# Seven joined block products for the last tokens of two batch pairs

## The chip, the cores and the metric

The kernel runs on one core of a Trainium2 chip. The metric is the device time of one execution in microseconds (us); lower is better. Below, PE is TensorE, DVE is VectorE, ACT is ScalarE, POOL is GpSimd and SP is SyncE.

## What is computed

The inputs are q, k and v of shape (8, 8, 576, 64): batch, heads, tokens, head dimension. A linear attention with a root-mean-square norm feeds a gated linear unit with a causal convolution of five taps:

```python
kv  = einsum('bhsd,bhse->bhde', k, v)
x   = einsum('bhsd,bhde->bhse', q, kv)
x   = x / sqrt(mean(x * x, -1) + 1e-6) * g_norm      # then heads side by side: (8, 576, 512)
gate = sigmoid(sum over k of conv_w[k] * x shifted by 4 - k tokens)
out  = (gate * (x @ w_val)) @ w_out                  # (8, 576, 512)
```

All of it is float32.

## The kernel before

The order of all work is written out by hand: `PLAN` is a list of 1245 steps, `name arguments @ buffers`, and the kernel's last loop calls the function of each step in turn. An engine runs its own instructions in that order; what stands between two engines is a wait for a semaphore. `@ 3 2` picks the numbered buffers of a step's new tiles: eight PSUM banks, and rooms in on-chip memory (`ot` has four, `gate` four, `xs` four, `w64` three, `x` three; `v0`, `v1`, `k0`, `k1` have one each and hold halves of one batch's v and k).

The batches go through these stages, overlapped with one another:

- `kv_product b i` (L478) multiplies k^T v, `kv_copy` takes the result out of PSUM; `load_q` and `turn_q` bring q and transpose it.
- `raw_pair b c` and `raw_tail b` (L553) multiply q by it, in 64x64 tiles, for two chunks of 128 tokens and for the last 64 tokens. `square`, `sums`, `powers` (POOL) and `normalise` (ACT, L638) make x.
- `turn_blocks` and `move_blocks` (L671, DMAs on SP's and POOL's queues) or, for the last 64 tokens, `turn_x` and `keep_x`, put x transposed into `xTs`. `halo` copies the tokens that the convolution reads from before a block.
- `gate_start`, `gate_tap` (L688, one DVE instruction per tap), `gate_end` make the gate of one quarter (128) of the channels.
- `val_fast b mj n` (L749) and `val_keep` make x @ w_val, `gated b jt` (L713) multiplies it by the gate, in place, in `gv`. `gv` holds three batches.
- the second product, w_out, goes by pairs of batches: pair i is batches 2i and 2i + 1. The first 512 tokens of a batch are four chunks of 128. Two chunks and two halves of w_out form two by two blocks, and seven products instead of eight give the result: `fast_product i p n` (L843), n = 0 to 6, p = 0 to 3 (two chunks each, p = 0, 1 of the first batch, 2, 3 of the second). Four of the seven use sums made by `token_sums i h m` (L818), for both p of a batch at once, and sums of weights made once. `fast_keep i p n` copies (n = 0, 1, 2, 6, on ACT, L856, L858, L860, L871) or adds (n = 3, 4, 5, on DVE, L854) what lies in PSUM into two `ot` tiles, and `store` sends these out with four DMAs each (L883).
- the last 64 tokens of the two batches of a pair together are 128 rows, chunk 8: `out_product i 8` (L787) makes them with plain products of 64 columns by 512, `keep_out` (L795) copies, `store i 8` sends.

All four pairs are done so. In PSUM, the b and c results of one (i, p) share a bank, except for (3, 3), the last. `store_last` and `store_part` split the last stores over SP's and ACT's queues.

Of the kernel before, what the change touches and what calls it, by code (L numbers as in the profile page):

```python
# [12 lines left out]
ALU = mybir.AluOpType  # L13
# [18 lines left out]
narrow_weight wval 1 0 @ 0; raw_half 0 1 0 @ 5; square 0 4 @ 0; sums 0 2; narrow_weight wval 0 3;
raw_half 0 1 1; sums 0 4; load_half v 2 1 @ 0; start_warm 2 384 @ 0; narrow_weight wval 1 1;
narrow_weight wval 0 4; powers 0 2; square 0 1 @ 1; narrow_weight wval 1 5 @ 0; narrow_weight wval 1 2;
narrow_weight wval 0 7; stage_weight wout 0 @ 2; turn_q_rows 1 3 @ 7; normalise 0 3 @ 0;
narrow_weight wval 1 3; turn_q_rows 1 2 @ 6; sums 0 1; sort_q 1 3 @ 1; turn_q_rows 1 1 @ 0;
load_half v 2 0 @ 0; narrow_weight wval 2 0 @ 1; turn_x 0 3 @ 1; narrow_weight wval 1 6 @ 1; powers 0 1;
normalise 0 4 @ 1; narrow_weight wval 2 1; turn_q_rows 1 0 @ 7; load_q 2 2; normalise 0 2 @ 2; turn_x 0 4 @ 4;
keep_x 0 3; narrow_weight wval 1 4; turn_x 0 2 @ 3; keep_x 0 4; narrow_weight wval 2 2;
narrow_weight wval 2 5 @ 2; kv_product 1 1 @ 1 4; narrow_weight wval 1 7; keep_x 0 2;  # L40
narrow_weight wval 2 6 @ 3; sort_q 1 1; val_product 0 1 1 @ 3; narrow_weight wval 3 0 @ 0;
narrow_weight wval 3 5 @ 0; halo 0; normalise 0 1 @ 0; narrow_weight wval 3 1; normalise 0 0 @ 1;
narrow_weight wval 2 3; narrow_weight wval 3 6 @ 1; turn_x 0 1 @ 0; narrow_weight wval 3 2; turn_x 0 0 @ 5;
narrow_weight wval 2 4; load_half k 2 1 @ 0; val_product 0 0 1 @ 2; keep_x 0 1; narrow_weight wout 1 5 @ 2;
keep_x 0 0; narrow_weight wval 2 7; narrow_weight wval 3 3; narrow_weight wout 1 0 @ 1;
narrow_weight wout 1 6 @ 0; gate_start 0 0 @ 0; kv_product 1 0; narrow_weight wval 3 4; gate_start 0 3 @ 1;
gate_tap 0 0 3; sort_q 1 2; turn_q_rows 1 4 @ 0; narrow_weight wval 3 7; val_product 0 0 0 @ 5; load_q 2 0;
gate_tap 0 0 2; keep_val 0 0 1; gate_tap 0 3 3; gate_start 0 1 @ 2; sort_q 1 4; val_sums 2;
val_product 0 3 0 @ 6; gate_tap 0 1 3; kv_copy 1 1; kv_copy 1 0; load_q 2 1; sort_q 1 0; gate_tap 0 0 1;
raw_tail 1 @ 0 2; gate_tap 0 3 2; raw_pair 1 3 @ 1 4; square 1 4 @ 2; narrow_weight wout 0 5 @ 3;  # L50
keep_val 0 0 0; gate_tap 0 0 0; val_product 0 2 1 @ 7; gate_start 0 2 @ 3; gate_tap 0 3 1; square 1 3 @ 0;
square 1 2 @ 1; sums 1 4 @ 1 1; gate_tap 0 2 3; narrow_weight wout 1 1; powers 1 4; load_half k 2 0 @ 0;
val_product 0 1 0 @ 5; sums 1 3; keep_val 0 1 1; stage_weight wout 3 @ 0; gate_end 0 0; gate_tap 0 1 2;
powers 1 3; narrow_weight wout 1 2; sums 1 2; narrow_weight wout 1 3; val_product 0 2 0 @ 3; gated 0 0;
keep_val 0 3 0; keep_val 0 2 1; gate_tap 0 2 2; normalise 1 4 @ 2; powers 1 2; narrow_weight wout 1 4;
normalise 1 3 @ 0; raw_pair 1 1 @ 7 6; turn_q 2 0 @ 0; stage_weight wout 2 @ 1; turn_q 2 2; turn_x 1 4 @ 0;
load_q 2 3; val_product 0 3 1 @ 2; gate_tap 0 3 0; keep_x 1 4; normalise 1 2 @ 1; gate_tap 0 2 1;
narrow_weight wout 0 6 @ 2; turn_x 1 3 @ 0; keep_val 0 3 1; gate_tap 0 1 1; load_q 3 1; turn_x 1 2 @ 1;
keep_val 0 1 0; square 1 1 @ 2; kv_product 2 0 @ 4 2; narrow_weight wout 0 0 @ 0; keep_x 1 3;
narrow_weight wout 1 7; keep_x 1 2; sums 1 1; kv_product 2 1; narrow_weight wout 0 1; gate_tap 0 1 0;  # L60
powers 1 1; square 1 0 @ 0; val_product 1 1 1 @ 5; narrow_weight wout 2 0 @ 1; load_half k 3 1 @ 0;
narrow_weight wout 0 2; narrow_weight wout 2 5 @ 1; load_half k 3 0 @ 0; narrow_weight wout 3 5 @ 3;
narrow_weight wout 0 3; sums 1 0; kv_copy 2 0; gate_tap 0 2 0; kv_copy 2 1; narrow_weight wout 2 1;
normalise 1 1 @ 2; powers 1 0; val_product 1 0 1 @ 0; narrow_weight wout 2 6 @ 0; narrow_weight wout 0 4;
turn_q 2 1; val_product 1 3 1 @ 1; halo 1; narrow_weight wout 2 2; narrow_weight wout 0 7; load_q 3 0;
keep_val 0 2 0; turn_q 2 3; keep_val 1 1 1; keep_val 1 0 1; weight_sums 0; normalise 1 0 @ 0; turn_x 1 1 @ 4;
load_q 3 2; narrow_weight wout 3 0 @ 0; raw_pair 2 3 @ 3 2; narrow_weight wout 3 6 @ 1; val_sums 0;
narrow_weight wout 2 3; raw_pair 2 1 @ 5 0; turn_q 3 1 @ 1; square 2 2 @ 1; turn_x 1 0 @ 6; square 2 3 @ 2;
narrow_weight wout 2 4; keep_x 1 1; val_product 1 2 1 @ 7; sums 2 2 @ 0 0; load_half v 3 0 @ 0; keep_x 1 0;
val_sums 1; gate_end 0 3; powers 2 2; load_half v 3 1 @ 0; sums 2 3; keep_val 1 3 1; gate_end 0 1; gated 0 3;  # L70
val_product 1 0 0 @ 4; gate_start 1 0 @ 0; narrow_weight wout 2 7; gate_end 0 2; powers 2 3; gated 0 1;
square 2 0 @ 0; gate_tap 1 0 3; val_product 1 1 0 @ 6; square 2 1 @ 1; turn_q 3 0; normalise 2 2 @ 1;
gated 0 2; load_q 3 3; val_product 1 2 0 @ 1; gate_tap 1 0 2; keep_val 1 2 1; keep_val 1 1 0; sums 2 1;
normalise 2 3 @ 2; load_q 4 0; turn_q 3 2; powers 2 1; val_product 1 3 0 @ 7; sums 2 0;
narrow_weight wout 3 1; token_sums 0 0 0 @ 2; keep_val 1 2 0; narrow_weight wout 3 2; turn_blocks 2 3;
kv_product 3 0 @ 2 6; powers 2 0; gate_tap 1 0 1; narrow_weight wout 3 3; token_sums 0 0 2 @ 1;
keep_val 1 3 0; fast_product 0 0 1 @ 3; normalise 2 1 @ 0; load_half k 4 0 @ 0; narrow_weight wout 3 4;
token_sums 0 0 1; fast_product 0 1 0 @ 1; turn_blocks 2 2; normalise 2 0 @ 2; fast_product 0 0 0 @ 7;
turn_q 3 3; kv_product 3 1; narrow_weight wout 3 7; load_q 4 2; fast_keep 0 0 1 @ 2; keep_val 1 0 0;
token_sums 0 0 3; fast_keep 0 0 0 @ 3; raw_tail 2 @ 0 5; gate_start 1 3 @ 1; turn_blocks 2 1;  # L80
fast_product 0 0 3; square 2 4 @ 2; turn_blocks 2 0; kv_copy 3 1; kv_copy 3 0; gate_start 1 1 @ 2;
fast_product 0 1 1 @ 4; sums 2 4; move_blocks 2 0; weight_sums 1; fast_keep 0 1 0 @ 0; raw_pair 3 1 @ 6 2;
weight_sums 2; powers 2 4; gate_tap 1 1 3; move_blocks 2 2; fast_product 0 0 2; gate_tap 1 0 0;
move_blocks 2 1; fast_product 0 1 2; gate_tap 1 3 3; fast_keep 0 0 2; fast_keep 0 1 1 @ 1; weight_sums 3;
fast_product 0 0 5; move_blocks 2 3; fast_keep 0 1 2; gate_tap 1 1 2; square 3 0 @ 1; fast_product 0 1 4;
# [845 lines left out]
```

## Time and profile before

| | us |
|---|---|
| median of 3 runs | 294.84 (294.74 to 295.19) |
| profiled execution, its own time | 295.31 |
| its span, first to last instruction | 293.5 |
| last instruction of the last k^T v (L478) ends | 190.7 |
| last `gated` ends on VectorE | 274.66 |
| last TensorE record starts | 288.9 |

Granted TensorE clock: 1.000. A float32 matmul of the program shows as two records on TensorE. Records overlap, so the time of a group is read from its start to the start of the next group. Rows of the timeline give start, length and group; rows of groups give the number of instructions, busy time and mean length in ns, and the idle time of the engine ahead of them with what ended it.

### The profile page before, as it was taken

The numbers are of one execution on the slowest core, as the hardware profiler recorded it, in microseconds if no ns is written. First come the engines' busy times: TensorE is split into PE (matmuls) and PEld (weight loads), VectorE is DVE, ScalarE is ACT, GpSimd is POOL, SyncE is SP. The second block draws the span as 40 slices with busy tenths as digits, with TensorE's granted clock in tenths as the row PEclk, the third lists the DMA queues.
The fourth block names the chain that finished last, engine by engine and source line by source line (L and its number), as shares of the span: only waits on it lengthen the run. The fifth ranks groups of instructions, "written<-read, shape, count | busy, mean of one in ns | idle before, by whom it ended". The sixth has DMA issues, their size and how long they took to land.

```text
span 293.5 us, 8687 instructions
## 1 busy us (share of the span) xinstructions
PE 285.4 (97%) x3281; PEld 225.4 (77%) x3281; DVE 268.6 (92%) x484; ACT 198.6 (68%) x621; POOL 122.3 (42%) x131
## 2 busy tenths in 40 slices
PE   6999999999999999999999999999999999999994
PEld 3777778877887868878887767888887588888583
DVE  1699999999999999999999999999998999999812
ACT  2899999999786767876477576658598434723330
POOL 3067064754594378322881748031592072000020
PEclk9999999999999999999999999999999999999999
DMA  7999999968586856947699689624552170221334
GB/s 262 379 388 409 288 252 271 276 223 237 152 223 174 253 129 189 339 129 202 167 252 282 145 233 296 209 61 120 134 129 74 47 170 0 57 54 36 97 102 125
DMA packets 32202, 55.51 MB, mean 189 GB/s; under 512 B 6231, under 2 KB 14679, under 8 KB 32161
## 3 DMA queue, kind: packets, MB, share of 16 engines
q1 hardware_dynamic: 29424, 49.50, 57.7%
q0 software_dynamic: 1760, 3.43, 5.2%
q10 hardware_dynamic: 976, 2.03, 1.9%
q8 instruction: 26, 0.43, 0.6%
q14 instruction: 16, 0.12, 0.1%
HBM read 39.21 MB, written 9.44 MB: 166 GB/s over the span
## 4 chain that ended last, share of the span: by engine, by line
PE 71%; ACT 10%; DVE 9%; DMA 5%; issue 1%; POOL 1%; SPq 1%; ACTq 0%; DVEq 0%
PE bank L843 29%; PE bank L749 28%; PE bank L787 5%; ACT x L638 4%; DMA v<-in_v_dram 4%; PE bank L478 4%; DVE gate L688 4%; PE bank L553 3%; PE bank L565 1%; DMA out_dram<-ot 1%; POOL rt L619 1%; DVE ss L609 1%; SPq L883 1%; DVE ot L424 1%; ACT gv L709 1%
## 5 line engine op out<-in xcount | busy, mean ns | idle before, releaser
L619 POOL TENSOR_TENSOR rt<-ss,mhalf 128x8 f32<-128x8 f32 (+3 forms) x38 | 73.0, 1935 | 78.7 <-DVE ss L609 78.6
L688 DVE SCALAR_TENSOR_TENSOR gate<-xT,cwT,gate 128x576 f32<-128x576 f32 x128 | 100.5, 808 | 0.2
L638 ACT ACTIVATE x<-bank,rt 128x64 f32<-128x64 f32 x252 | 55.8, 366 | 4.0 <-POOL rt L619 3.7
L843 PE MATMUL bank<-wsum,w 128*128 128x256 f32 x192 | 47.6, 381 | 0.1
L671 POOL DMA_DIRECT2D xT<-y x48 | 26.5, 557 | 41.5 <-DVE gv L756 13.5
L843 PEld LDWEIGHTS bank<-wsum,w 128*128 128x128 f32 x192 | 36.0, 190 | 6.4 <-issue 0.8
L749 PE MATMUL bank<-xs,vsum 128*128 128x288 f32 x144 | 37.1, 407 | 0.0
L749 PEld LDWEIGHTS bank<-xs,vsum 128*128 128x128 f32 x144 | 27.3, 190 | 7.3
L700 PE MATMUL bank<-xT,wval 128*128 128x288 f32 x128 | 32.5, 408 | 0.0
L843 PE MATMUL bank<-wout,gv 128*128 128x256 f32 x128 | 32.0, 381 | 0.0
L700 PEld LDWEIGHTS bank<-xT,wval 128*128 128x128 f32 x128 | 23.7, 190 | 6.2 <-ACT xT L657 0.2
L695 ACT ACTIVATE gate<-gate 128x576 f32<-128x576 f32 x32 | 23.0, 725 | 7.9 <-DVE gate L688 7.8
L843 PEld LDWEIGHTS bank<-wout,gv 128*128 128x128 f32 x128 | 24.1, 190 | 3.5
L602 ACT ACTIVATE sq<-bank 128x256 f32<-128x256 f32 (+1 forms) x70 | 21.7, 401 | 6.2 <-PE bank L553 5.8
L682 ACT ACTIVATE gate<-xT,cwT 128x576 f32<-128x576 f32 x32 | 25.2, 803 | 0.9 <-DVE gv L713 0.9
L749 PE MATMUL bank<-xT,wval 128*128 128x288 f32 x96 | 25.7, 406 | 0.0
L713 DVE TENSOR_TENSOR gv<-gv,gate 128x576 f32<-128x576 f32 x32 | 23.5, 747 | 2.0 <-ACT gate L695 1.4
L609 DVE TENSOR_REDUCE ss<-sq 128x8 f32<-128x520 f32 (+1 forms) x40 | 24.8, 625 | 0.3 <-ACT sq L602 0.3
L854 DVE TENSOR_TENSOR ot<-bank,ot 128x256 f32<-128x256 f32 (+1 forms) x33 | 17.4, 535 | 8.0 <-PE bank L843 4.0
L749 PEld LDWEIGHTS bank<-xT,wval 128*128 128x128 f32 x96 | 18.2, 190 | 4.5
L860 ACT COPY ot<-bank 128x256 f32<-128x256 f32 x16 | 6.0, 375 | 22.2 <-PE bank L843 22.2
L678 POOL COPY xT<-xT 128x124 f32<-128x124 f32 x32 | 18.7, 622 | 4.7 <-ACT xT L657 3.5
(91 smaller groups left out, 466.5 us busy)
## 6 DMA issues: line engine op xcount, KB each, us to landing
qs<-in_q_dram SPq DMA_DIRECT2D x96, 140.0 KB, 4.0
out_dram<-ot SPq DMA_DIRECT2D x134, 64.0 KB, 1.7
k<-in_k_dram SPq DMA_DIRECT2D x14, 576.0 KB, 5.1
v<-in_v_dram SPq DMA_DIRECT2D x12, 576.0 KB, 5.3
xT<-y SPq DMA_DIRECT2D x48, 64.0 KB, 2.7
xT<-y POOLq DMA_DIRECT2D x48, 64.0 KB, 2.6
y<-in_moe_w_val_dram SPq DMA_DIRECT2D x4, 512.0 KB, 12.6
w<-in_moe_w_out_dram SPq DMA_DIRECT2D x4, 512.0 KB, 8.1
```

Of the source, the lines that this page charges most:

```text
L602: nc.scalar.activation(out=sq[:, r * n // 2:(r + 1) * n // 2, 0:D], in_=raw.rearrange("p (h e) -> p h e", e=D), func=AF.Square)
L609: nc.vector.reduce_sum(out=st["ss", b][:, FIRST[c]:FIRST[c] + n], in_=st["sq", b, c][:, 0:n], axis=AX.X)
L619: nc.gpsimd.tensor_tensor(out=st["rt", b][:, which], in0=st["ss", b][:, which], in1=mhalf[:, which], op=ALU.pow)
L638: nc.scalar.activation(out=x[:, to * D:(to + 1) * D], in_=raw[:, h * D:(h + 1) * D], func=AF.Copy, scale=root[:, to:to + 1])
L671: (nc.sync if i % 2 else nc.gpsimd).dma_start(out=xTs[b % 2][i * TB:(i + 1) * TB, :, first:first + P], in_=y[a * TB:(a + 1) * TB, i])
L682: nc.scalar.activation(out=gate[:], in_=xTs[b % 2][:, jt, HALO:SX], func=AF.Copy, scale=cwT[:, K - 1, jt:jt + 1])
L688: nc.vector.scalar_tensor_tensor(out=gate[:], in0=xTs[b % 2][:, jt, tap * TB:tap * TB + S], scalar=cwT[:, tap, jt:jt + 1], in1=gate[:], op ...
L695: nc.scalar.activation(out=gate[:], in_=gate[:], func=AF.Sigmoid)
L700: nc.tensor.matmul(val[:], wval[:, kc, jt * P:(jt + 1) * P], xTs[b % 2][:, kc, HALO + n * SV:HALO + (n + 1) * SV], start=(kc == 0), stop=( ...
L713: nc.vector.tensor_tensor(out=both, in0=both, in1=st["gate", b, jt][:], op=ALU.mult)
L749: nc.tensor.matmul(st[bank, "val", b, mj][:], weights_[:, k], tokens()[:, k], start=(n in (0, 1, 3) and k == 0), stop=(k == NK // 2 - 1), ...
L843: nc.tensor.matmul(st[bank, i, p], tokens()[:, k], weights_[:, k], start=((n < 2 or n == 3 and ("bc", i, p) not in st) and k == 0), stop=( ...
```

## The change

Everything up to `kv_product 7 0`, the last k^T v, keeps its order on every engine. Behind it:

- `out_product`, `keep_out` and `store` of chunk 8 are gone for pairs 2 and 3. Instead `keep_tail b` (ACT) copies the last 64 tokens of batches 4 to 7 from `gv` into two tiles of 128 tokens (in `k0` and `k1`), and these two form one more group of two by two blocks, called pair 5, p = 0: four `token_sums`, seven `fast_product`, six `fast_keep` and the stores of two tiles.
- the output sums of (1, 3), (2, 3), (3, 1) and (5, 0) stand in `v0` and `v1` instead of `ot`.
- `move_blocks` is split into a step for POOL's queue and a step for SP's, so that the plan can place them apart.
- all steps behind `kv_product 7 0` have a new order.

```diff
     FAST_OUT = 0
     PAIRED_Q = (0, 1)
+    SPARE = ((1, 3), (2, 3), (3, 1), (5, 0))
+    APART = ((B // 2 - 1, 2 * NV - 1),)
...
-    def move_blocks(b, a):
+    def move_blocks(b, a, e):
...
-        for i in range(HB):
-            (nc.sync if i % 2 else nc.gpsimd).dma_start(
+        for i in range(1 - e, HB, 2):
+            (nc.gpsimd if e else nc.sync).dma_start(
...
+    def keep_tail(b):
+
+        i = b // 2
+        if ("tail", i) not in st:
+            st["tail", i] = new(("wexp", "wexp", "k0", "k1")[i], [P, NK, P], FP32, f"tail{i}")
+        first = b % GVS * S + SF
+        nc.scalar.copy(out=st["tail", i][:, :, b % 2 * T:(b % 2 + 1) * T], in_=gv[:, :, first:first + T])
...
+        if i < B // 2:
+            block = lambda r, k: gv[:, k, begin:begin + SF].rearrange(
+                "p k (m r t) -> p k m r t", m=2, r=2)[:, :, :, r, :]
+            done = lambda m: st["sums", i, h, m // 2][:, m % 2]
+        else:
+            block = lambda r, k: st["tail", 2 * (i - B // 2) + r][:, k]
+            done = lambda m: st["sums", i, h, m // 2][:, m % 2, :, 0]
...
-        chunk = lambda r, k: lambda: gv[:, k, begin + r * P:begin + (r + 1) * P]
+        chunk = lambda r, k: lambda: (
+            gv[:, k, begin + r * P:begin + (r + 1) * P] if i < B // 2 else st["tail", 2 * (i - B // 2) + r][:, k])
...
-        elif bank != "a" and (i, p) == (B // 2 - 1, 2 * NV - 1):
+        elif bank != "a" and (i, p) in APART:
...
-            st["ot", i, 2 * p + row] = new("ot", [P, C], FP32, f"ot{i}_{2 * p + row}")
+            tag = f"v{row}" if (i, p) in SPARE else "ot"
+            st["ot", i, 2 * p + row] = new(tag, [P, C], FP32, f"ot{i}_{2 * p + row}")
...
+            first = 2 * i
+            if i >= B // 2:
+                first, bb, n = 4 * (i - B // 2) + 2 * c, j // 2, NJ * HB + j % 2
```

Pieces of the new order that the prediction speaks of, first around batch 7's raw products and batch 5's gates:

```diff
+fast_product 1 2 3; gate_tap 5 2 1; store 1 5; val_fast 6 1 0 @ 0; val_fast 6 0 1 @ 1; x_sums 6 1 @ 0;
+fast_keep 1 2 5; store 1 4; val_keep 6 1 0; gate_tap 5 2 0; gate_end 5 2; turn_blocks 7 3; turn_blocks 7 2;
+turn_blocks 7 1; move_blocks 7 3 1; move_blocks 7 3 0; gated 5 2; val_fast 6 0 2; gated 5 3; x_sums 6 2 @ 1;
```

and from the last gates to the end (the end before was `... fast_product 3 3 6; fast_keep 3 3 5; store_last 3 6 1; store_last 3 6 0; fast_keep 3 3 6; store_part 3 7 0 1 2 4; store_part 3 7 0 0 0 2`):

```diff
+val_keep 7 1 3; gate_tap 7 2 0; gate_end 7 0; fast_product 3 1 5; fast_product 3 0 3; gated 7 1; gated 7 0; gated 7 3;
+fast_product 3 3 0 @ 0; gate_end 7 2; gated 7 2; keep_tail 7; fast_keep 3 3 0 @ 3; fast_product 3 2 0 @ 5;
+fast_keep 3 2 0 @ 0; token_sums 3 1 0 @ 2; fast_product 3 2 1 @ 4; fast_keep 3 1 5; store 3 2; token_sums 5 0 0 @ 1;
...
+fast_keep 5 0 6; store_last 5 1 1; fast_keep 3 3 6; fast_product 5 0 5; store_last 5 1 0; fast_product 5 0 3;
+fast_keep 5 0 5; store_part 3 7 0 1 2 4; fast_product 3 3 3 @ 7; fast_keep 3 3 3; store_part 3 7 0 0 0 2;
+store_last 5 0 0; store_last 5 0 1; fast_product 3 3 5; fast_keep 3 3 5; store_last 3 6 1; store_last 3 6 0
```

More of the change, by code (lines that the diff above doesn't have):

```diff
@@ L52 @@
[L52 to L60, printed above, removed]
+load_q_rows 0 1; load_q_rows 0 0; load_half v 0 0 @ 0; load_half k 0 0 @ 0; load_half v 0 1 @ 0; load_half k 0 1 @ 0;
@@ L70 @@
[L70 to L74, printed above, removed]
@@ L80 @@
[L80 to L84, printed above, removed]
@@ new lines @@
+token_sums 0 0 1; fast_product 0 1 0 @ 1; turn_blocks 2 2; normalise 2 0 @ 2; fast_product 0 0 0 @ 7; turn_q 3 3;
+kv_product 3 1; narrow_weight wout 3 7; load_q 4 2; fast_keep 0 0 1 @ 2; keep_val 1 0 0; token_sums 0 0 3;
+fast_keep 0 0 0 @ 3; raw_tail 2 @ 0 5; gate_start 1 3 @ 1; turn_blocks 2 1; fast_product 0 0 3; square 2 4 @ 2;
+turn_blocks 2 0; kv_copy 3 1; kv_copy 3 0; gate_start 1 1 @ 2; fast_product 0 1 1 @ 4; sums 2 4; move_blocks 2 0 1;
+move_blocks 2 0 0; weight_sums 1; fast_keep 0 1 0 @ 0; raw_pair 3 1 @ 6 2; weight_sums 2; powers 2 4; gate_tap 1 1 3;
@@ L100 @@
-gated 1 3; turn_blocks 3 1; raw_tail 3 @ 3 4; kv_product 4 0; val_keep 2 1 6; gated 1 2; square 3 4 @ 0;
-turn_blocks 3 2; out_product 0 8 @ 1; sums 3 4; kv_copy 4 1; kv_copy 4 0; turn_blocks 3 3; val_keep 2 0 6;
-powers 3 4; gate_start 2 0 @ 2; token_sums 0 1 0 @ 0; move_blocks 3 2; gate_start 2 2 @ 1; turn_q 4 3;
-normalise 3 4 @ 2; move_blocks 3 1; turn_q 4 1; gate_tap 2 3 3; raw_pair 4 3 @ 2 7; token_sums 0 1 1;
-move_blocks 3 0; gate_tap 2 2 3; raw_pair 4 1 @ 6 5; square 4 3 @ 2; gate_tap 2 2 2; keep_out 0 8 @ 0;
@@ L120 @@
-normalise 4 2 @ 1; val_fast 3 1 4; gate_tap 2 3 0; store 0 7; fast_keep 0 2 5; val_fast 3 0 1 @ 6; turn_q 5 2;
-gate_end 2 3; kv_product 5 1 @ 0 5; x_sums 3 3 @ 3; gate_start 3 0 @ 1; gated 2 3; raw_tail 4 @ 7 2;
-load_half k 6 1 @ 0; kv_product 5 0; gated 2 1; square 4 4 @ 1; store 0 4; val_keep 3 0 1; sums 4 4;
-val_fast 3 0 5; turn_q 5 0; powers 4 4; kv_copy 5 0; fast_keep 0 2 6; gate_start 3 1 @ 0;
-token_sums 1 0 0 @ 1; fast_product 1 1 0 @ 0; turn_blocks 4 2; token_sums 1 0 1; load_q 5 3;
@@ L145 @@
[L145 to L148 removed]
+x_sums 2 0 @ 0; val_fast 2 0 0 @ 0; fast_keep 0 1 5; x_sums 2 1 @ 1; store 0 2; raw_pair 3 3 @ 1 2; val_keep 2 0 0;
@@ new lines @@
+val_fast 2 0 3 @ 3; normalise 3 3 @ 1; val_keep 2 1 4; load_q 4 3; val_keep 2 0 4; val_fast 2 0 5; gate_tap 1 3 1;
+val_keep 2 0 3; val_fast 2 0 6; gate_tap 1 3 0; val_fast 2 1 6; gated 1 1; load_q 5 1; gate_end 1 3; val_keep 2 0 5;
+normalise 3 2 @ 0; kv_product 4 1 @ 6 5; gated 1 3; turn_blocks 3 1; raw_tail 3 @ 3 4; kv_product 4 0; val_keep 2 1 6;
+gated 1 2; square 3 4 @ 0; turn_blocks 3 2; out_product 0 8 @ 1; sums 3 4; kv_copy 4 1; kv_copy 4 0; turn_blocks 3 3;
+val_keep 2 0 6; powers 3 4; gate_start 2 0 @ 2; token_sums 0 1 0 @ 0; move_blocks 3 2 1; move_blocks 3 2 0;
@@ new lines @@
+val_fast 3 1 1 @ 6; sums 4 2; gate_tap 2 1 1; powers 4 2; val_fast 3 0 4; val_keep 3 1 1; turn_blocks 4 3;
+val_keep 3 1 2; val_fast 3 1 5; gate_tap 2 1 0; gated 2 2; fast_product 0 2 5; gate_end 2 1; val_keep 3 1 5;
+fast_keep 0 3 6; normalise 4 2 @ 1; val_fast 3 1 4; gate_tap 2 3 0; store 0 7; fast_keep 0 2 5; val_fast 3 0 1 @ 6;
+turn_q 5 2; gate_end 2 3; kv_product 5 1 @ 0 5; x_sums 3 3 @ 3; gate_start 3 0 @ 1; gated 2 3; raw_tail 4 @ 7 2;
+load_half k 6 1 @ 0; kv_product 5 0; gated 2 1; square 4 4 @ 1; store 0 4; val_keep 3 0 1; sums 4 4; val_fast 3 0 5;
@@ new lines @@
+gated 4 2; square 6 2 @ 1; sums 6 3; turn_q 7 0 @ 1; fast_product 1 3 0 @ 6; load_q 7 2; kv_copy 7 1;
+token_sums 2 0 0 @ 1; fast_product 2 1 0 @ 1; sums 6 2; kv_copy 7 0; token_sums 2 0 1; keep_tail 4 @ 0;
+token_sums 2 0 2 @ 0; turn_blocks 6 0; gate_start 5 3 @ 2; fast_product 2 0 0 @ 5; fast_product 2 0 1 @ 0;
+fast_keep 1 3 0 @ 0; fast_keep 2 1 0 @ 0; gate_start 5 0 @ 3; store 1 8; fast_product 2 1 1 @ 4; fast_keep 2 0 0 @ 1;
+fast_product 2 0 2; fast_product 2 1 2; powers 6 3; token_sums 1 1 1; fast_product 1 3 2; normalise 6 3 @ 2;
@@ new lines @@
+gate_tap 5 0 2; normalise 7 2 @ 0; fast_product 1 3 5; fast_keep 1 3 4; sums 7 3; store 2 3; gate_tap 5 0 1;
+store 2 0; raw_tail 7 @ 2 7; square 7 4 @ 0; gate_tap 5 1 1; store 2 1; fast_product 1 3 6; fast_keep 1 3 6;
+gate_tap 5 0 0; gate_end 5 0; gate_tap 5 1 0; fast_product 1 2 2; fast_keep 1 2 2; halo 6; store 1 7; sums 7 4;
+fast_product 1 2 1 @ 5; gate_end 5 1; fast_keep 1 2 1 @ 2; turn_blocks 7 0; gated 5 0; gate_start 6 3 @ 3; gated 5 1;
+fast_product 1 3 3; fast_keep 1 3 5; powers 7 3; gate_tap 5 3 3; powers 7 4; store 1 6; gate_tap 5 2 3;
```

335 lines of the change are left out of this document (159 added, 176 removed).

## The prediction

> **What bounds the kernel now.** I read the page first (shares of the engines, then the slices), then the busy time by stretches behind the last k^T v, then TensorE's timeline there, the waits, and the end of the chain.
>
> ```profile
> span 293.5 us, 8687 instructions
> PE 285.4 (97%) x3281; PEld 225.4 (77%) x3281; DVE 268.6 (92%) x484; ACT 198.6 (68%) x621; POOL 122.3 (42%) x131
> ...
> PE   6999999999999999999999999999999999999994
> ...
> DVE  1699999999999999999999999999998999999812
> ```
>
> TensorE (PE) and VectorE (DVE) are both near full, and DVE empties only in the last two slices. All steps up to the last k^T v (`kv_product 7 0`) are issued in the same order on every engine after the change, so the first 190.66 us can't differ. The stretches behind it:
>
> ```profile
> core 0: us, PE busy (x) PEld busy (x) DVE busy (x) ACT busy (x) POOL busy (x), PEclk, DMA share, GB/s
> 190.66:200.00 9.34, 9.34 (x50) 8.25 (x44) 9.30 (x18) 6.04 (x20) 3.33 (x2) 1.00 0.33 87
> ...
> 260.00:270.00 10.00, 10.00 (x47) 8.60 (x46) 10.00 (x18) 3.35 (x8) 0.00 (x0) 1.00 0.20 51
> ...
> sum 98.64, PE 98.54 PEld 78.53 DVE 87.68 ACT 50.89 POOL 26.31; mean PE 9.85 PEld 7.85 DVE 8.77 ACT 5.09 POOL 2.63
> ...
> 188.66:274.66 86.00, 85.94 (x649) 70.43 (x640) 83.51 (x139) 49.05 (x144) 24.26 (x31) 1.00 0.33 83
> ```
>
> PE is busy in 98.54 of the 98.64 us from the last k^T v to its own end, at full granted clock. Busy alone doesn't prove that it is at its pace, so I read the starts in its timeline (columns: start, length, group):
>
> ```profile
> 188.57 1.11 PE L553 MATMUL bank<-kv,qT 64*64 64x64 f32 x64
> 189.50 1.23 PE L478 MATMUL bank<-v,k 64*64 64x64 f32 x72
> ...
> 201.99 1.03 PE L843 MATMUL bank<-wsum,gv 128*128 128x256 f32 x4
> 202.95 2.09 PE L553 MATMUL bank<-kv,qT 64*64 64x64 f32 x128
> 204.97 1.13 PE L843 MATMUL bank<-wsum,gv 128*128 128x256 f32 x4
> 205.94 1.89 PE L843 MATMUL bank<-wout,gv 128*128 128x256 f32 x8
> 207.67 3.95 PE L843 MATMUL bank<-wsum,w 128*128 128x256 f32 x16
> 211.45 1.03 PE L843 MATMUL bank<-wout,w 128*128 128x256 f32 x4
> ...
> 227.29 3.65 PE L787 MATMUL bank<-wout,gv 128*64 128x512 f32 x16
> 230.87 0.47 PE L553 MATMUL bank<-kv,qT 64*64 64x64 f32 x16
> ...
> 275.05 3.65 PE L787 MATMUL bank<-wout,gv 128*64 128x512 f32 x16
> 278.64 1.99 PE L843 MATMUL bank<-wsum,w 128*128 128x256 f32 x8
> ...
> 288.24 1.03 PE L843 MATMUL bank<-wsum,gv 128*128 128x256 f32 x4
> ```
>
> Two block products (eight records) take 207.67 - 205.94 = 1.73 us, so one product is 0.865 us. The only visible loss is at 207.67: four products take 3.78 us instead of 3.46. So PE's work sets the end of this section, and a change pays only what it takes off PE, unless it makes PE wait.
>
> **The change, part by part.** *The tails.* The two tail steps of pairs 2 and 3 go: 230.87 - 227.29 = 3.58 us and 278.64 - 275.05 = 3.59 us, 7.17 us together. Their 64-column records already run nearly two at a time (16 in 3.58 us is 0.22 each, though one is 0.6 long), so less is saved than the number of records suggests. Added are seven products, 7 x 0.865 = 6.06 us. PE: -1.11 us.
>
> *Changes of tile size.* The one product before the two raw pairs at 202.95 takes 0.96 us, the one after them 0.97, 0.10 over each; the pairs take 2.02, where a pair between other 64-wide work takes 0.93 (188.57 to 189.50). One excursion to 64-wide tiles thus costs 0.10 + 0.16 + 0.10 = 0.36 us. Before has the two raw pairs of batch 7 in one excursion, the raw tail joined to a tail step, and the last tail step on its own. After has three separate excursions. Before: 0.36, some 0.4 for the joined one and 0.2 for entering and leaving the last tail step, 0.96; after: 3 x 0.36 = 1.08. I take +0.15, between 0 and one excursion, 0.36.
>
> *Output buffers.* The waits of this section:
>
> ```profile
> ACT ot L856 <- DMA out_dram<-ot: 3.2, 2, 2.3
> ...
> PEld bank L843 <- ACT ot L856: 0.5, 1, 0.5
> ...
> DVE gv L713 <- ACT gate L695: 1.4, 2, 1.0
> DVE gv L713 <- ACT gv L770: 0.4, 1, 0.4
> ...
> DVE ot L854 <- PE bank L843: 4.0, 4, 2.8
> DVE ot L854 <- ACT ot L795: 3.9, 1, 3.9
> ```
>
> The loss at 207.67 has its cause here: ScalarE's first copy of a product (L856) waits for an `ot` buffer until a store has landed, and PE waits for the bank. After, the sums of (1,3), (2,3), (3,1) and the tails stand in the two v buffers, free by then, which adds two buffers to four. I take the 0.32 us as gone; the bounds are 0.32 (gone) and 0 (it returns elsewhere). PE in all: -1.11 + 0.15 - 0.32 = -1.28 us.
>
> *What the joined tails cost elsewhere.*
>
> ```profile
> L854 DVE TENSOR_TENSOR ot<-bank,ot 128x256 f32<-128x256 f32 x18 | 7.5, 416 | 7.6 <-ACT ot L795 3.9 <-PE bank L843 3.6
> ...
> L854 DVE TENSOR_TENSOR ot<-bank,ot 128x512 f32<-128x512 f32 x15 | 10.1, 678 | 0.4 <-PE bank L843 0.4
> ...
> L856 ACT COPY ot<-bank 128x256 f32<-128x256 f32 x16 | 6.2, 402 | 7.7 <-PE bank L843 4.5 <-DMA out_dram<-ot 3.2
> ...
> L657 ACT ACTIVATE xT<-bank 128x256 f32<-128x256 f32 x8 | 3.3, 413 | 1.9 <-PE bank L650 1.9
> ...
> L795 ACT COPY ot<-bank 128x512 f32<-128x512 f32 x4 | 2.4, 588 | 2.8 <-PE bank L787 2.8
> ```
>
> DVE gets four token sums of 256 elements and one add of 256 (0.42 each by the nearest row), and one add of 512 (0.68): 5 x 0.42 + 0.68 = 2.8 us. All stand behind the last `gated`, where DVE has 7.9 us of waits for PE and for the old tail copy; that hides them. If that cover is gone, they cost up to 2.8. ScalarE gets four tail copies and four product copies (8 x 0.41 = 3.3 us) and loses two copies of 0.588: +2.1 us on an engine that is busy 50.89 of 98.64. The tail copies wait for `gated`; behind them in ScalarE's order are product copies that the next bank needs, and `keep_tail 7` directly follows the last `gated`, before the copies of products that have not yet run. Cost nothing. GpSimd loses four store issues and ScalarE's queue gets four; SP's four of `store 2 8` come at the end instead, behind stores whose data are there earlier.
>
> *The order.* `move_blocks` is the same DMAs in two steps. For batch 6 only one store stands on SP's queue among them, for batch 7 none that still waits; POOL has no store left to wait behind. `raw_tail 7` moves ahead of batch 6's products: behind 21 block products and two raw pairs it starts near 211 instead of 230.87, and its sums and powers follow it; the taps of batch 5 move behind batch 7's sums. DVE is the engine this strains. Counted in both orders, the same 133 steps stand on DVE from `gate_tap 4 2 0` (188.66) to the last `gated` of batch 7, which ended at 274.66: 83.51 us busy and 2.49 idle by the stretch quoted above. Back to back they overlap a little:
>
> ```profile
> 272.02 1.44 DVE L713 TENSOR_TENSOR gv<-gv,gate 128x576 f32<-128x576 f32 x2
> ```
>
> Two in 1.44 us are 0.72 each, where one alone is 0.75 or more; each break loses some 0.08 beside its idle time, so I put the loss at 2.5 to 3.2 us. Without waits the last gate would end at 271.4 to 272.2, and the first two that are needed, two gates earlier, at 270.0 to 270.8. PE, 1.28 us earlier than its 288.24 + 0.865, ends its slot at 287.8; from `fast_product 3 3 0`, the first that needs batch 7's gates, 20 products follow (17.3 us), so it comes there at 270.5. That is a close race, -0.3 to +0.5 us. It is won only if the new order takes DVE's waits away. I looked at each: `gated 5 3` waited 0.97 of the 1.4 us for its sigmoid, queued on ScalarE behind a `normalise`; in the new order, two taps, an x sum, an add, three `turn_blocks` and another `gated` stand between its last tap and it. `gated 7 2` waited 0.4 for the copy of `val_fast 7 0 6`, which now runs before several other products; `gated 6 3` has another tap, `gated 6 1` and an add in between. I find no step that obviously waits, and charge 0.2 us of new PE waits, with 0 and 1.0 as the bounds: 0.2 is nearest to the 0.3 that the present order leaves to PE.
>
> *The end.*
>
> ```profile
> 289.28 0.02 issue
> 289.30 0.42 DVE ot L871
> ...
> out_dram<-ot SPq DMA_DIRECT2D x10, 64.0 KB, 1.9
> ...
> out_dram<-ot SPq DMA_DIRECT2D x4, 32.0 KB, 1.7
> out_dram<-ot ACTq DMA_DIRECT2D x4, 32.0 KB, 1.8
> out_dram<-ot ACTq DMA_DIRECT2D x2, 64.0 KB, 2.0
> ```
>
> Both orders end with one DVE instruction of 256 elements and two DMAs on each of two queues. Those are whole rows now (64 KB) instead of half rows (32 KB), and land in 1.9 and 2.0 instead of 1.7 and 1.8 us: +0.2, or 0 if the landing overlaps.
>
> The sum: -1.28 + 0.2 + 0.2 = -0.88 us. The profiled execution took 295.31 us, 1.81 outside its span of 293.5, and is 0.47 above the median of the runs, 294.84; taking 0.88 from the span gives 292.6, and from the median 293.96, say **294.0 us**.
>
> **The rivals.** *DVE stays late (slower).* If DVE loses its 2.5 to 3.2 us in the new order too, batch 7's first gates end two gates before 274.66, at 273.3. With 0.1 us to PE and 17.3 us of products the slot ends at 290.7 instead of before's 289.1: +1.6, and +0.2 for the end, 296.6 us. It turns to slower once DVE waits for 0.8 to 1.6 us. For it: 10.00 busy of 10.00 at 260 to 270, and that more gate-dependent PE work is left for the end (19 products, 16.4 us, against 14 and a tail step, 15.7). Against: ScalarE, which caused most of these waits, has its gate work further ahead. The Trainium skill, Perfetto Trace Analysis, "Identifying the Most-Contended Engine", says to judge TensorE's headroom by the weight-load share and not by matmul busy time, and VectorE by occupancy; at 77% and 92% that names VectorE, so relieving TensorE should bring nothing and 2.8 us of added DVE work should show. By that rule this rival's time holds; the starts every 0.865 us speak for TensorE in this section, and the trace so far does not agree with the rule.
>
> *The gain is eaten (no change).* The 0.32 us wait returns at another buffer, PE waits 0.5 and the excursion costs its full 0.36: -1.11 + 0.36 + 0.5 + 0.2 = -0.05, 294.8 us. For it: spare slack is a few tenths everywhere.
>
> *No new wait at all.* -1.28 with no longer landing: 293.6 us.
>
> **How the numbers follow.** Forecast with or without the 0.2 of waits, 0.65; gain eaten 0.15; DVE late 0.2. A difference of 0.2% (0.59 us) is about what a measurement of this kernel tells from no change. The forecast holds nearly all of faster, 0.66; same 0.14; slower 0.20. The range reaches from 293.3 (1.28 and 0.26 more from runs' spread and shorter switches) to 295.6, half of the way into the DVE rival, which leaves out about 2 in 10.
>
> **What would show it.** Right: no L787 after 190.66, 28 more L843 records, PE starts 0.865 us apart throughout, its last product some 1.1 us earlier, the wait of L856 for a store gone, DVE's idle time ahead of the last gate under 0.8 us, two 64 KB DMAs on each queue last. Wrong: a gap in PE's starts before `fast_product 3 3 0` or `3 0 0` released by DVE (the first rival); PE waiting for L856 or L858 again (the buffers); a longer way from PE's end to the span's end than 4.2 us by more than 0.3.

## The result, and the profile after

The kernel after the change takes 293.79 us (median of 6 runs, 293.65 to 293.87), the kernel before took 294.93 beside it (6 runs, 294.74 to 295.19): a ratio of 0.996, 95% interval 0.9947 to 0.9973, or 1.1 us less. The forecast was 294.0 us in 293.3 to 295.6.

In the profile after, block products stand in L851 (before: L843), copies and adds of products in L863 to L880 (L854 to L871), `gated` in L707, the raw products in L547, `val_fast` in L743, `token_sums` in L825, `keep_tail` in L793. The page, and two rows of the busy time by stretches, with the columns of the prediction:

```profile
span 292.0 us, 8669 instructions
PE 285.1 (98%) x3277; PEld 228.5 (78%) x3277; DVE 270.3 (93%) x490; ACT 199.9 (68%) x627; POOL 122.2 (42%) x127
...
DVE  1699999999999999999999999999999999999822
```

```profile
188.46:271.38 82.92, 82.92 (x635) 69.52 (x625) 82.86 (x138) 48.89 (x146) 25.69 (x31) 1.00 0.34 87
190.53:288.04 97.51, 97.51 (x566) 81.52 (x566) 89.34 (x151) 51.03 (x154) 25.69 (x31) 1.00 0.34 85
```

From the end of the last k^T v to its own end TensorE is busy in all of 97.51 us. VectorE does the 133 steps up to the last `gated` in 82.92 us, where it took 86.00 before, and is idle for 0.06 of them instead of 2.49. TensorE's timeline (start, length, group, and in brackets an idle time ahead of it with what ended it):

```profile
189.30 1.23 PE L472 MATMUL bank<-v,k 64*64 64x64 f32 x72
...
200.06 1.03 PE L851 MATMUL bank<-wout,gv 128*128 128x256 f32 x4
201.02 1.16 PE L547 MATMUL bank<-kv,qT 64*64 64x64 f32 x64
202.11 1.13 PE L851 MATMUL bank<-wsum,gv 128*128 128x256 f32 x4
203.08 1.03 PE L851 MATMUL bank<-wsum,w 128*128 128x256 f32 x4
...
252.43 4.62 PE L851 MATMUL bank<-wsum,w 128*128 128x256 f32 x20
256.89 1.13 PE L743 MATMUL bank<-xs,vsum 128*128 128x288 f32 x4
...
269.62 2.75 PE L851 MATMUL bank<-wout,gv 128*128 128x256 f32 x12
272.26 3.69 PE L851 MATMUL bank<-wsum,w 128*128 128x256 f32 x16
275.79 1.03 PE L851 MATMUL bank<-wout,w 128*128 128x256 f32 x4
...
287.01 1.03 PE L851 MATMUL bank<-wout,w 128*128 128x256 f32 x4
```

The way from the start of the last k^T v group to the start of the last product is 287.01 - 189.30 = 97.71 us, against 288.24 - 189.50 = 98.74 before: 1.03 us less. In the kernels e8 to e12 below, whose work up to there is the new kernel's, the same way took 97.70 to 97.72 us, so this number varies little between runs. No row behind the last k^T v has a bracket. The first 190 us, the same work in both, ended 0.20 us earlier; in the other profiled runs of the same work they ended between 190.43 and 191.01, so that is spread between runs. The rest of the difference of the spans, 1.47 us, is the end: 0.24 us. This last number is less certain: the medians differ by 1.14 us only, because the profiled execution of the kernel before took 295.31, 0.38 above its median.

VectorE at the last gates, and the waits behind the last k^T v (in the waits: who waited on which tile, for whom, us in total, times, longest):

```profile
268.63 2.75 DVE L707 TENSOR_TENSOR gv<-gv,gate 128x576 f32<-128x576 f32 x4
271.42 0.69 DVE L825 TENSOR_TENSOR w<-gv 128x512 f32<-128x512 f32 x1
```

```profile
DVE v L863 <- PE bank L851: 4.4, 2, 3.1
...
DVE ot L863 <- DMA out_dram<-ot: 0.4, 1, 0.4
...
PEld bank L851 <- DVE v L863: 0.2, 1, 0.2
```

The four last gates end at 271.38 (before: 274.66), and no row names a copy on ScalarE that waits for a store. VectorE's waits for TensorE all lie behind the gates.

### The profile page after: what moved, and what is told of

Read it like the earlier page. It is cut to its first block, busy times and chain, and to the rows that moved or that the text cites. A ratio compares the mean times of both kernels' runs of the same rounds, so it can differ in the third digit from the quotient of the medians.

```text
span 292.0 us, 8669 instructions
## 1 busy us (share of the span) xinstructions
PE 285.1 (98%) x3277; PEld 228.5 (78%) x3277; DVE 270.3 (93%) x490; ACT 199.9 (68%) x627; POOL 122.2 (42%) x127
## 4 chain that ended last, share of the span: by engine, by line
PE 75%; DVE 9%; ACT 8%; DMA 4%; POOL 1%; issue 1%; ACTq 0%; DVEq 0%
PE bank L851 35%; PE bank L743 28%; PE bank L547 4%; DMA v<-in_v_dram 4%; PE bank L472 4%; DVE gate L682 4%; ACT x L632 3%; PE bank L781 2%; PE bank L559 1%; POOL rt L613 1%; DVE ss L603 1%; DVE ot L418 1%; ACT gv L703 1%; ACT sq L596 1%; DVE x L622 1%
## 5 line engine op out<-in xcount | busy, mean ns | idle before, releaser
L851 PE MATMUL bank<-wsum,w 128*128 128x256 f32 x204 | 49.3, 381 | 0.0
L851 PEld LDWEIGHTS bank<-wsum,w 128*128 128x128 f32 x204 | 38.1, 190 | 6.1 <-ACT v L865 0.3
L743 PE MATMUL bank<-xs,vsum 128*128 128x288 f32 x144 | 37.6, 407 | 0.0
L743 PEld LDWEIGHTS bank<-xs,vsum 128*128 128x128 f32 x144 | 27.3, 190 | 7.1
L851 PE MATMUL bank<-wout,gv 128*128 128x256 f32 x128 | 32.0, 381 | 0.0
L851 PEld LDWEIGHTS bank<-wout,gv 128*128 128x128 f32 x128 | 24.1, 190 | 3.6
L743 PE MATMUL bank<-xT,wval 128*128 128x288 f32 x96 | 26.2, 406 | 0.0
L707 DVE TENSOR_TENSOR gv<-gv,gate 128x576 f32<-128x576 f32 x32 | 22.9, 741 | 0.0
L743 PEld LDWEIGHTS bank<-xT,wval 128*128 128x128 f32 x96 | 18.2, 190 | 4.4
L672 POOL COPY xT<-xT 128x124 f32<-128x124 f32 x32 | 20.8, 689 | 1.2 <-ACT xT L651 0.6
L547 PEld LDWEIGHTS bank<-kv,qT 64*64 64x64 f32 x1008 | 16.4, 135 | 5.0 <-ACT x L632 2.8
L547 PE MATMUL bank<-kv,qT 64*64 64x64 f32 x1008 | 18.4, 221 | 0.2 <-ACT x L632 0.2
```

The source lines that it names most:

```text
L547: nc.tensor.matmul(st["raw", b, c][r][cols, to * D:(to + 1) * D], st["qT", b][rows, hp, first:first + D], kvs[b % 2][rows, hp, :], start=T ...
L743: nc.tensor.matmul(st[bank, "val", b, mj][:], weights_[:, k], tokens()[:, k], start=(n in (0, 1, 3) and k == 0), stop=(k == NK // 2 - 1), ...
L851: nc.tensor.matmul(st[bank, i, p], tokens()[:, k], weights_[:, k], start=((n < 2 or n == 3 and ("bc", i, p) not in st) and k == 0), stop=( ...
```

## The experiments

Times of a set are compared with runs of the kernel before on the same chip (medians 294.8 to 295.1). Line numbers in rows of the experiments are the new kernel's less 200, except in the kernel built from the old order.

**Is it the joined products or the order? e1 and e2.** e1 keeps the old order and only joins the tails; e2 keeps the new order and takes the old tail steps.

```diff
 (e1, against the kernel before)
-out_product 2 8; ... keep_out 2 8; ... store 2 8
+keep_tail 4 @ 0; keep_tail 5
...
 gated 7 2
+keep_tail 6 @ 0; keep_tail 7
-out_product 3 8; ... keep_out 3 8; ... store_side 3 8
+SPARE = ((5, 0),)
 (then the steps of pair 5, p = 0, between the last products of pair 3)
```

> The joined tails alone, in the old order (their products, sums and stores put where the old tail steps stood and after, only (5, 0) in the v buffers). Theory, that VectorE's last gates set the pace of the end: they end near 274.5 as before, the sums of batch 7's chunks near 277, and behind them come 18 products of 0.865 us instead of 12 and a tail step, so the time rises by 1 to 3.7 us, to 296 to 298.6. Rival, that TensorE's work alone counts: 1.1 us less than before, 293.8.

Measured: 299.89 us, ratio 1.0167 (1.0149 to 1.0185), above both expectations. TensorE's timeline:

```profile
227.27 0.48 PE L347 MATMUL bank<-kv,qT 64*64 64x64 f32 x16
229.04 1.24 PE L543 MATMUL bank<-xs,wval 128*128 128x288 f32 x4 [1.29 <-DVE xs L528]
...
273.64 1.03 PE L651 MATMUL bank<-wout,k 128*128 128x256 f32 x4
275.88 1.97 PE L651 MATMUL bank<-wsum,w 128*128 128x256 f32 x8 [1.22 <-DVE w L625]
```

The first wait stands where the tail step of pair 2 was: its 3.58 us of TensorE work had covered an x sum on VectorE. The second is the first sums behind the gates. With three smaller ones TensorE's way to its last product is 3.9 us longer than in the kernel before, on 1.1 us less work.

```diff
 (e2, against the new kernel)
-val_fast 6 1 3 @ 4; ... keep_tail 5; val_keep 6 1 3
+out_product 2 8 @ 4; keep_out 2 8 @ 0; store 2 8
...
+val_fast 6 1 3 @ 4; val_keep 6 1 3 (four products later: its bank is taken)
...
+out_product 3 8 @ 6; keep_out 3 8 @ 0 (behind fast_product 3 2 4)
-(all steps of pair 5, and keep_tail)
+store_last 3 8 0; store_last 3 8 1 (from v0 instead of ot)
```

> The new order alone, with the old tail steps (the one of pair 2 in place of a product of batch 6 that moves behind four others, the one of pair 3 in place of the joined products near the end). Theory, that TensorE is at its pace throughout the new order: two tail steps and their switches, 7.4 us, for seven products, 6.06, make it 1.3 us slower than the changed kernel, 295.1, no better than before. Rival, that the order made the gain: no more than 294.0.

Measured: 298.21 us, ratio 1.0106 (1.009 to 1.0121), again above both. The waits:

```profile
DVE gv L550 <- PE bank L543: 2.8, 2, 2.3
...
PE bank L651 <- DVE gv L507: 0.2, 1, 0.2
```

VectorE waited 2.3 us for the `val_fast` that had to move, so this measures a piece of the experiment as well as the tails. It does show how tight the order is: one step later by four products costs VectorE 2.3 us. Neither half gains by itself, but part of the 3 to 5 us that they lose against the kernel before is due to how they were put together; these two don't split the gain cleanly.

**What does the order have to cover? e7.** The kernel before, without its tail steps of pairs 2 and 3:

```diff
-out_product 2 8; ... keep_out 2 8; ... store 2 8
-out_product 3 8; ... keep_out 3 8; ... store_side 3 8
```

> The kernel before without the tail steps of pairs 2 and 3, their copies and stores (the last 64 tokens of batches 4 to 7 are not written): 7.17 us less on TensorE, two copies less on ScalarE, VectorE as before. Theory (in the old order the gates and sums on VectorE come next, so the joined products could gain only with the new order): TensorE waits for gates and sums for most of what is taken off, 292.5 to 293.5. Rival (TensorE's work alone set the time before): 287.7.

Measured: 294.17 us (292.04 to 295.43 in 10 runs), ratio 0.9962 (0.9939 to 0.9985). TensorE's timeline, and two stretches with the granted clock (the number behind the five engines):

```profile
229.38 1.24 PE L541 MATMUL bank<-xs,wval 128*128 128x288 f32 x4 [1.38 <-DVE xs L526]
...
276.23 3.27 PE L635 MATMUL bank<-wsum,w 128*128 128x256 f32 x8 [2.08 <-DVE w L610]
279.29 1.45 PE L635 MATMUL bank<-wout,gv 128*128 128x256 f32 x4
```

```profile
272.00:276.00 4.00, 2.15 (x10) 1.54 (x9) 3.84 (x7) 1.27 (x4) 0.00 (x0) 1.00 0.45 114
276.50:279.90 3.40, 3.40 (x10) 2.73 (x9) 1.00 (x2) 0.36 (x1) 0.00 (x0) 0.53 0.53 136
```

7.17 us less on TensorE bring 0.8 us in the median and 3.0 in the best run: TensorE waits for an x sum, then for the first sums behind the gates. The rival (287.7) is out; the median lies above the theory's range too, since TensorE ran part of the time at a lower granted clock (the second stretch), of which more below. So in the old order VectorE came next by far. That a shorter TensorE could therefore pay only in another order is argued from e1 and e7; no run isolates it.

**Which engine sets the new order? e3 to e6.** e3 leaves out two products ahead of the last gates, e4 two behind them (their part of the output is missing), e5 and e6 make one token sum on VectorE once or three times more.

```diff
 (e3)                          (e4)
-fast_product 2 2 3           -fast_product 5 0 3
-fast_product 3 0 3           -fast_product 3 2 3
 (e5, e6)
 token_sums 3 0 2 @ 0
+token_sums 3 0 2 (e5: once; e6: three times)
```

> The changed kernel without two products that run ahead of batch 7's last gates, (2, 2) n = 3 and (3, 0) n = 3, 1.73 us of TensorE; the sums that they belong to lack that part. Theory, that VectorE and TensorE arrive at the last gates together: TensorE then waits for the gates and the first sum, and the time falls by 0 to 0.3 us, 293.5 to 293.8. Rival, that TensorE alone sets the time: 1.73 less, 292.1.

Measured: 294.29 us, ratio 0.997 (0.9959 to 0.9982). Nothing is gained. TensorE and VectorE there:

```profile
267.26 1.91 PE L651 MATMUL bank<-wout,w 128*128 128x256 f32 x8
270.33 1.99 PE L651 MATMUL bank<-wout,gv 128*128 128x256 f32 x8 [1.17 <-DVE gv L507]
```

```profile
268.86 2.75 DVE L507 TENSOR_TENSOR gv<-gv,gate 128x576 f32<-128x576 f32 x4
```

The gates stand where they stood (268.86 against 268.63; the first 190 us took 0.23 longer in this run), and what was taken off TensorE is waited out in front of them and of the first sum: the way from the last k^T v to the last product is 97.71 us, as in the new kernel. So TensorE does wait for VectorE, as the theory of a tie said, and the two products bring nothing. The time lies 0.5 us above the theory's range: beside the 0.23 us of the first 190, the profiled run took 0.23 longer from the last add on VectorE to the end.

> The changed kernel without two products that run behind the last gates, (5, 0) n = 3 and (3, 2) n = 3, 1.73 us of TensorE; the sums that they belong to lack that part. Theory, that behind the gates only TensorE paces: 1.73 less, 292.1. Rival, that VectorE's sums or the stores pace this stretch too: less than 1.0 gained, 292.8 or more.

Measured: 292.89 us, ratio 0.9923 (0.9909 to 0.9938), 0.9 us below the new kernel and just inside the rival's range. TensorE reached its last product 1.73 us sooner behind the last k^T v, all of the two products, but the span ends 4.19 us behind the last add on VectorE instead of 3.53 (the table below). The timeline of the end:

```profile
286.64 0.42 DVE L663 TENSOR_TENSOR ot<-bank,ot 128x256 f32<-128x256 f32 x1 [0.44 <-PE bank L651]
287.10 0.80 ACTq L695 DMA_DIRECT2D out_dram<-ot  x2
287.31 0.78 SPq L695 DMA_DIRECT2D out_dram<-v  x2
288.19 0.88 SPq L695 DMA_DIRECT2D out_dram<-ot  x2
```

ScalarE's queue issues its last pair right behind the last add, SP's 1.09 us later: the two stores ahead of it had to wait for a semaphore that an earlier store still held. So behind the gates TensorE sets the pace up to its last product, and the queue of late stores, the rival, takes 0.66 us of what that gains.

> The new kernel with the same token sum of pair 3 made once more, to the same result: +0.60 us on VectorE ahead of batch 7's gates. Made three times more it cost TensorE one wait of 2.07 us, and the granted clock was 0.5 for 3.4 us behind it. Theory (no slack on VectorE, and a short wait brings no lower clock): TensorE waits 0.5 to 0.9 us in all at full granted clock, 294.2 to 294.7. Rival (a slack of some tenths): 293.8 to 294.0.

Measured: 294.63 us, ratio 0.9992 (0.9983 to 1.0001), inside the theory's range: 0.60 us of VectorE work takes the gain away. The wait stands where the prediction had not looked, 11 us ahead of the last gates:

```profile
257.01 1.13 PE L543 MATMUL bank<-xs,vsum 128*128 128x288 f32 x4
258.60 1.78 PE L651 MATMUL bank<-wsum,gv 128*128 128x256 f32 x7 [0.45 <-DVE v L663]
```

A product waits for a bank that an add on VectorE has yet to empty. In the new kernel the weight load waits 0.2 us for the same add (the last row of its waits above) and the product not at all, so there is next to no slack at that place.

> The new kernel with one token sum of pair 3 (0.60 us on VectorE, ahead of batch 7's gates) made three times more, to the same result: +1.8 us on VectorE, nothing on any other engine. Theory (VectorE has no slack left ahead of the last gates, 0.4 us at the most): TensorE waits 1.4 to 1.8 us at the first products of the second half of batch 7, and the time is 295.2 to 295.6, so the whole gain is gone. Rival (VectorE is still 1 us or more ahead of TensorE): at most 294.4.

Measured: 297.3 us (296.12 to 298.2), ratio 1.0069 (1.0048 to 1.009), above the theory's range:

```profile
256.94 1.13 PE L543 MATMUL bank<-xs,vsum 128*128 128x288 f32 x4
259.98 2.63 PE L651 MATMUL bank<-wsum,gv 128*128 128x256 f32 x8 [1.91 <-DVE v L663]
```

```profile
257.60:260.00 2.40, 0.49 (x3) 0.04 (x2) 2.40 (x5) 0.00 (x0) 0.00 (x0) 1.00 0.00 0
261.20:264.60 3.40, 3.40 (x9) 2.53 (x8) 2.37 (x5) 1.86 (x4) 0.00 (x0) 0.50 0.38 96
```

The same wait, now 1.91 us, and behind it 3.4 us at a granted clock of 0.50, in which TensorE starts 9 records; at full clock, one every 0.216 us, it would start 15. The runs fall into two groups by it: the three whose mean granted clock is 0.997 or 0.998 took 296.12 to 296.76, the three at 0.993 took 297.83 to 298.2. Without the clock the cost is 2.3 to 3.0 us for 1.8 us of VectorE work (why it is more than 1.8 is not shown), with it 4 and more.

**What paces the end? e8 to e12.** All of them change only how the last tiles are stored.

```diff
 (e8)
+store_rows 3 6 0 1; store_rows 3 6 0 0        (ahead of fast_product 3 3 5)
-store_last 3 6 1; store_last 3 6 0
+store_rows 3 6 1 1; store_rows 3 6 1 0        (one DMA of 2 x 32 rows per queue)
 (e9: e8, and the stores of (3, 7) and of pair 5 by store_rows too)
 (e10)
+store_part 3 6 0 1 2 4; store_part 3 6 0 0 0 2 (ahead of fast_product 3 3 5)
-store_last 3 6 1; store_last 3 6 0
+store_part 3 6 1 1 2 4; store_part 3 6 1 0 0 2
 (e11)
-store_last 5 0 0
+store_pool 5 0 0 2                             (GpSimd's queue)
 (e12)
-store_part 3 7 1 1 2 4; store_part 3 7 1 0 0 2
-store_part 3 7 0 1 2 4; ... store_part 3 7 0 0 0 2
+store_last 3 7 1; ... store_last 3 7 0
```

> The new kernel, but tile (3, 6)'s half of 256 columns that is ready first is stored ahead of the last product, and the last half goes as one DMA of 64 rows on each queue instead of two DMAs of 32 rows. Theory (the 4.4 us from the last TensorE record to the end are paced by issues and semaphore waits on SP and ScalarE behind the last add): 0.4 to 0.8 us less, 293.0 to 293.4. Rival (the landing of the last bytes alone): no change, 293.7 to 293.9.

> As the kernel with one DMA per queue for the last half, and the late stores of tile (3, 7) and of the joined tails also as one DMA of 64 rows each: six DMAs less on each queue. Theory (SP's queue waits for earlier stores on reused semaphores): another 0.1 to 0.4 us, 292.7 to 293.2. Rival: larger DMAs land later and it is slower than the kernel with the last half alone, 293.4 or more.

Measured: 299.09 us (ratio 1.0136, 1.0123 to 1.0149) and 311.15 (1.0542, 1.0529 to 1.0556). Both theories and both rivals are off by far. A stretch of e8 behind all work (the last two columns: busy share of the 16 DMA engines, GB/s), and the same of the new kernel:

```profile
290.50:295.50 5.00, 0.00 (x0) 0.00 (x0) 0.00 (x0) 0.00 (x0) 0.00 (x0) 0.76 0.13 41
```

```profile
288.90:290.70 1.80, 0.00 (x0) 0.00 (x0) 0.00 (x0) 0.00 (x0) 0.00 (x0) 1.00 0.63 166
```

0.13 of 16 engines is two. A DMA written as two blocks of 32 rows (their rows lie apart in the output, so they don't merge) ran on two DMA engines, and the last byte came 7.6 us behind the last add instead of 2.3. The Trainium skill, DMA: Bandwidth & Descriptors, section "Why a DMA increments its semaphore by 16 and not by 1", says that a DMA is spread over the largest number of engines, 16 at most, that divides the slowest dimension of both sides; that of the output side is two here, and the trace agrees. These two runs thus say nothing on issues and semaphores.

> The new kernel, but tile (3, 6) is stored as half rows, as the kernel before stored its last tile: the half that is ready first ahead of the last product, then the other half, each by two DMAs of 32 rows on each queue. The last DMAs carry 32 KB instead of 64, and there are four more of them. Theory of the prediction (64 KB land 0.2 us later): 293.6. Rival (the end is paced by issues that wait for semaphores of earlier stores): 0.2 to 0.6 us more, 294.0 to 294.4.

> The new kernel, but SP's two stores of the first tile of the joined tails (issued at 287.07 and 287.94 us) go by GpSimd's queue, which is empty. Theory (SP's last pair, issued 0.46 us behind ScalarE's, is held up by these and their semaphores): 0.2 to 0.5 us less, 293.3 to 293.6. Rival (GpSimd's issues take longer and land later, or the closing checks wait all the same): 293.8 or more.

> The new kernel, but tile (3, 7) is stored as whole rows by four DMAs of 64 KB instead of half rows by eight of 32 KB: four DMAs fewer in the last 7 us. Theory (late stores wait to issue for semaphores of stores that have yet to land, so fewer of them let the last pair go sooner): SP's last pair is issued 0.2 to 0.45 us sooner and the time is 293.3 to 293.6, below the new kernel's. Rival (the last add, ScalarE's pair and the landing set the end, and the larger stores land later): 293.8 or more.

Measured: e10 294.37 us (ratio 0.9981, 0.9973 to 0.999), e11 295.76 (1.003, 1.0019 to 1.0042), e12 294.19 (0.9971, 0.9959 to 0.9984). None is below the new kernel's ratio of 0.996. The end of each, from the times of the instructions and of the DMA packets in the traces:

```
          last add  SP's last    ScalarE's last  last   SP's last  span
          ends      pair issued  pair issued     byte   check      ends
before    289.72    289.90       289.98          291.68  292.61    293.50
after     288.50    288.99       288.53          290.78  291.14    292.03
e4        287.07    288.19       287.10          290.01  290.37    291.26
e10       288.60    289.01, 290.11  289.09, 289.73  291.22  291.83  292.72
e11       288.66    288.69       288.69          290.80  291.61    294.02
e12       288.78    288.81       288.81          290.80  291.53    292.42
```

"SP's last check" is the start of the last of nine instructions with which SP, behind its last issue, waits for the DMA semaphores one after the other, in the order of their numbers, some 0.06 us each where nothing is left to wait for. In e12 SP's pair goes out with ScalarE's, as the theory said, and the last byte lands 2.02 us behind the last add, against 2.28 in the new kernel. But one of the last stores has the semaphore that is checked third, and six more checks come behind its landing: from the last byte to the last check it takes 0.73 us, against 0.36 in the new kernel, whose last stores have the numbers that are checked last. The 0.26 us gained are given back, and the time lies in the rival's range. e10, with four more DMAs, issues its last at 290.11, because its semaphore came free only then: the rival's case, and the rival's time. In e11 SP's pair goes at once too, but GpSimd, which had issued two DMAs late, stays in its drain instruction from 288.25 for 4.98 us, and the close of the program waits for it. So what was said of the issues shows in each trace, and each time something else at the end takes more than it gave.

## Why the prediction was right, and where not

*The bound.* Right. TensorE's way to the last product is 1.03 us shorter, against -1.28 + 0.2 = -1.08.

*Tails and tile sizes.* Summed over TensorE's records by the time to the next start, the tail steps lost 7.17 us, the block products went from 61.05 us (280 records) to 67.23 (308), and the raw products from 2.43 to 2.59. 28 records at 0.2163 (0.865 / 4) are 6.06. The first excursion, in the rows above, costs 0.96 + 1.09 + 0.97 against 0.865 + 0.93 + 0.865: 0.36, as worked out.

*Buffers.* Right: the 0.32 us at 207.67 are gone, and ScalarE's copies wait for no store. No run has the two added buffers alone.

*New waits.* 0.27 for 0.2: 0.14 us at 254 (five products in 256.89 - 252.43 = 4.46 us instead of 4.32), by a copy on ScalarE, and 0.12 between 269.62 and 275.79, where products wait for the first sum of pair 3's second half. What is then left of -1.03 is +0.13 for the changes of tile size, where 0.15 was charged.

*VectorE.* Right, by little. The last gate ended at 271.38 (271.4 to 272.2), the second at 270.05 (270.0 to 270.8), TensorE came at 270.48 (270.5). The rival in which VectorE stays late did not happen, but its turning point was put too far off: not 0.8 to 1.6 us but 0.6 (e5), since the place without slack is an add 11 us ahead of the gates, and with a wait of 1.9 us the clock can add to it (e6). The rule of the Trainium skill, Perfetto Trace Analysis, "Identifying the Most-Contended Engine", named VectorE: this holds ahead of the last gates, where 1.73 us off TensorE brought nothing (e3), and not behind them, where they came off the time of its last product in full (e4). The first tail step was taken out ahead of the gates, and this paid only because the new order took 2.4 us of idle time off VectorE as well.

*The end.* The step that failed: +0.2 was forecast and -0.24 came. The last byte did come later, 2.28 us behind the last add instead of 1.96, +0.32, but only in part by the mechanism of the prediction. From the issue of the later last pair to the last byte it took 1.79 us (290.78 - 288.99) instead of 1.70 (291.68 - 289.98): +0.09. The other 0.23 are SP's last pair, issued 0.49 us behind the last add where the later of the two pairs of before went out 0.26 behind it, because it waited for the semaphore of an earlier store. In e12, where both pairs go at once, the four 64 KB DMAs do take 1.99 us to the last byte, 0.29 more than before, and it comes 2.02 behind the add, only 0.06 later than before. What the prediction left out is the way from the last byte to the end: 1.82 us before, 1.25 after, 0.57 less that nobody planned. The order of SP's closing checks is 0.31 of it: before, the check that passed last for want of a landing was the fourth of nine, at 292.30, with five more behind it until 292.61; after, it is the ninth, at 291.14. The other 0.26 are that this check passed 0.62 us behind the last byte before and 0.36 after; why is not shown. With 0.44 us less at this term the forecast of 294.0 would have been 293.6; it came out at 293.79. So that the time came this close to the forecast is partly luck: the new kernel's end gained what no term had, and the spread between the runs of the kernel before is as large as this term.

## What to carry to other kernels

Read the bound of each stretch, and test it from both sides: here taking work off TensorE paid only behind the last gates, adding 0.6 us to VectorE cost as much as the change had brought, and the two engines met with less than half a microsecond to spare at 258, 270 and 272 us. A step removed from the critical engine was also cover for others (e1, e7); look up what is late next before it goes. At the end of a kernel count, beside the landing of the last bytes, the waits of late DMAs for semaphores of earlier ones and the closing checks: they are worth some tenths either way, and they move with any change to the last stores.

## What the runs showed of the hardware

- A TensorE wait of about 2 us can cost twice. Behind waits of 1.91 us (e6) and 2.08 us (e7) the granted clock fell to 0.50 for 3.41 us by the trace's clock record; behind waits of 1.17 to 1.38 us (e1, e3, e7) it did not. By the mean clock, three of six runs of e6 had it. The Trainium skill, TensorE: Matmul & The Clock Gate, Part 1, gives the same half clock and a window of 3413 ns, which agrees, but asks for an idle window of that length before the clock falls; here 2 us were enough. The length of a wait is not all that counts, though. In the clock records a fall comes a whole number of steps of 3.413 us behind the start of the record (75 in e6, 79 in e7, 84 in e8), and in the step just ahead of it TensorE was idle for 1.91 us (e6), 2.08 (e7) and all 3.41 (e8, at the end, where the fall at 293.10 came 5.1 us behind the last product's end). A step with 1.97 us idle, at the end of the kernel before, brought none, so the limit lies near 2 us and is not sharp in these figures. A wait of 2 us that falls into two steps would then cost no clock; that this is what parted the runs of e6 is likely but not shown, since one trace of it was kept.
- DMAs of two blocks that don't merge ran on two of the 16 DMA engines, at 41 GB/s in all (e8); DMAs of 32 rows moved 166 GB/s at the same place.
- A DMA issue waits when the earlier DMA with the same semaphore has not landed; with 13 (new kernel) and 12 (e4) DMAs issued on the two queues in the 4 us up to the last, this held up SP's last pair against ScalarE's by 0.46 us (new kernel) and 1.09 us (e4).
- SP's closing checks go by number, some 0.06 us each, and in e11, whose GpSimd queue issued its last DMAs at 287.81 and 288.33, GpSimd's drain held the close up by 1.6 us behind them (291.68 to 293.28). In the kernel before the same drain took 5.30 us from 284.00 and held up nothing.
